# The stores of an FFT's first stage: one per pair of blocks in place of two

## The chip, the cores and the metric

The kernel runs on one core of a Trainium2 chip. The metric is the device time of one execution in microseconds (us), the median of several runs. The profile is that of one further execution.

The engines are TensorE (PE; its weight loads are PEld), VectorE (DVE), ScalarE (ACT), GpSimd (POOL) and SyncE (SP), which here only issues transfers. Each works through its own queue of instructions in order. ACT's queue holds arithmetic and the issues of transfers (DMAs) mixed.

## The reference

The input x has 2048 positions and 448 channels. It is normalised over the channels, and two branches of the result are added to it: a long convolution along the positions (an S4D state-space layer, whose kernel has 2048 taps per channel and comes from 256 modes), and a gated linear unit with 1792 hidden columns.

```python
x = A_u
xn = _layernorm(x, axis=-1)
# branch A: K from the modes, then a causal convolution by FFT of length 4096
P = jnp.exp((A * dt[:, None])[:, :, None] * pos[None, None, :])
K = 2.0 * jnp.einsum("dn,dnl->dl", C, P).real
Kf, Uf = jnp.fft.rfft(K, L2), jnp.fft.rfft(u_t, L2)
y = jnp.fft.irfft(Uf * Kf[None, :, :], L2)[:, :, :L]
# branch B
h = _sigmoid(xn @ w_gate) * (xn @ w_up)
return x + (y + xn * D_skip) + h @ w_down
```

## The kernel before, in words

**Two branches at once.** Two generators are advanced in turn: conv() (L1020) for branch A and glu() (L731) for branch B. They share all engines. The framework then orders the instructions of each engine with a scheduler that estimates how long each takes; tc.issue_after and high_priority (hp) bind a few of them. So an edit of one transfer can move instructions on every engine.

**Positions.** The 2048 positions are taken as 16 blocks of 128 rows. Normalised blocks are called xn (first 8) and xt (last 8).

**The first stage of x.** The 4096-point transform of x is done in two steps. In the first, x_first_stage (L277) multiplies one group g of 32 rows of a block by a table wx, which gives 64 spectral rows. It does so for a pair of blocks, b and b+1: block b into the upper 64 rows of a PSUM tile, block b+1 into the lower 64. ACT copies the tile to SBUF, and DMAs issued from ACT store it to x1_d in DRAM, laid out as (half of the channels, row(b, g), 64 spectral rows, 224 channels). row(b, g) (L274) is 32 * (b // 4 % 2) + 8 * g + 4 * (b // 8) + b % 4, so b and b+1 of a pair stand next to each other, and g and g+1 stand 8 apart.

- x_spec (L283) does this for the pairs of blocks 0 to 7, four calls. Two groups share a buffer (x1a, x1b, x1c in turn); the copies are L294 and L296, the stores L301.
- pair_first (L681) does it for the pairs of blocks 8 to 15, four calls, one group at a time; the copies are L689, the stores L691.

**The second step** reads x1_d much later, from 514 us on, in spectra() (loads at L875, issued from SP), and multiplies the spectra of x and K.

**K.** prep (L345) computes the modes' magnitudes and phases on ACT and DVE in 112-row tiles, at the same time as x_spec. kgen (L461) then takes the channels in 56 steps: a matmul makes phases (tr, L542), ACT turns them into sines and cosines in four instructions (S, L548 to L551), DVE multiplies by magnitudes me and mf (Et at L602 and L603, Ft at L604), TensorE contracts Ft with Et into ko (L616), and every fourth step a first stage of K's own transform follows (kp, kq, L566; stored by L574 from ACT).

**Branch B.** Weights are loaded from SP (wraw, L640 and L642; one buffer), cast on ACT to a rounded part wh (L760), and DVE takes the rest wl (L764), which also frees wraw for the next load. Rounded part and rest are multiplied apart. gate (L696) makes two PSUM banks (L710); ACT takes a tanh (th, L718), DVE forms hf (L721), ACT rounds it (hh, L726), DVE takes the rest (hl, L728). The down projection po (L823) follows, drained by DVE into acc (L828). All banks called gu and po are four buffers used in turn. While the last group of hidden columns of the first half is done, pair_norm, pair_turn (transposes L212, with copies xh and xr on ACT, L218, L221 and L224, and rests xl and xr on DVE, L219, L222 and L225) and pair_first are woven in for blocks 8 to 15.

**Transfers.** All DMAs issued from SP and ACT take eight completion semaphores in turn, in the order in which the scheduler puts them, and an issue waits until the DMA that had its semaphore before has landed.

Of the kernel before, what the change touches and what calls it, by code (L numbers as in the profile page):

```python
# [39 lines left out]
H = D // 2  # L40
# [90 lines left out]
def s4d_glu_kernel(ctx, tc, io):  # L131
    nc = tc.nc
# [9 lines left out]
    x1_d = dram.tile([2, NB, 64, H], F32, name="x1_d")  # L142
# [131 lines left out]
    def row(b, g):  # L274
        return 32 * (b // 4 % 2) + 8 * g + 4 * (b // 8) + b % 4

    def x_first_stage(to, xn, g):  # L277

        s = slice(32 * g, 32 * g + 32)
        for i in range(2):  # L280
            nc.tensor.matmul(to[64 * i : 64 * i + 64], wx[s], xn[i][s], start=True, stop=True)

    def x_spec(xn, b0):  # L283

        x1s_ = []
        for _ in range(2):
            x1s_.append(slots[("x1a", "x1b", "x1c")[x1s[0] % 3]])
            x1s[0] += 1
        ps = psc[-1].tile([128, 2, 512], F32, name="tr", bufs=1)
        kk = [psc[-1].tile([128, 512], F32, name=n, bufs=1) for n in ("ko", "kp")]  # L290
        with tc.issue_after(glu_mm[0].ins):
            for j in range(4):
                x_first_stage((ps[:, j] if j < 2 else kk[j - 2])[:, :D], xn, j)
        nc.scalar.copy(x1s_[0], ps[:, :, :D])  # L294
        for j in range(2):
            nc.scalar.copy(x1s_[1][:, j], kk[j][:, :D])  # L296
        for p in range(2):
            for i in range(2):
                r = row(b0 + i, 2 * p)
                for h in range(2):  # L300
                    nc.scalar.dma_start(  # L301
                        x1_d[h, r : r + 9 : 8].rearrange("r k d -> k r d"),
                        x1s_[p][64 * i : 64 * i + 64, :, H * h : H * h + H],
                    )
        yield 2 * WX

    def exp(ex, ki, fr, pl):
# [373 lines left out]
    def pair_first(b, xns):  # L681

        x1 = pg.tile([128, 2, D], F32, name="x1", tag="wraw", bufs=1)
        pss = [psg.tile([128, 512], F32, name="gu", bufs=4) for _ in range(4)]
        for g in range(4):
            x_first_stage(pss[g][:, :D], xns, g)
        for g in range(4):
            to = x1[:, g] if g < 2 else pg.tile([128, D], F32, name="x1", tag="rd", bufs=RB)
            nc.scalar.copy(to, pss[g][:, :D])  # L689
            for i in range(2):  # L690
                nc.scalar.dma_start(  # L691
                    x1_d[:, row(b + i, g)].rearrange("h k d -> k h d"),
                    to[64 * i : 64 * i + 64].rearrange("k (h d) -> k h d", h=2),
                )

    def gate(w, xs, to, between=None, behind=False):  # L696
        wh, wl = w
# [33 lines left out]
    def glu():  # L731
        for half in range(2):
# [4 lines left out]
            for fs_ in ORDER[half]:  # L737
# [8 lines left out]
                if cross:  # L746
                    xts = {b: pair_load(b) for b in range(8, 16, 2)}
                    step = lambda f_, b: f_(b, xts[b])
                    mid = [(pair_norm, 8), None, (pair_first, 8), (pair_first, 10)]
                    end = [(), ((pair_turn, 8), (pair_norm, 10)), ((pair_turn, 10), (pair_norm, 12)), ((pair_turn, 12), (pair_norm, 14))]  # L750
                    downs = {(0, 0): (pair_first, 12), (0, 1): (pair_turn, 14), (0, 3): (pair_first, 14)}
# [268 lines left out]
    def conv():  # L1020
        with tc.tile_pool(name="psk", bufs=1, space=PSUM) as ps_, tc.tile_pool(
# [9 lines left out]
            with tc.tile_pool(name="pst", bufs=1, side="right", reuse_waits="tile") as pst:  # L1031
# [54 lines left out]
                while preps:  # L1086
                    for p in list(preps):
                        try:
                            with tc.issue_after(hfs[max(0, len(hfs) - LAG)].ins):
                                next(p)  # L1090
                        except StopIteration:
                            preps.remove(p)
                    yield WP
                    n += 1
                    if n in (2, 3):
                        if n == 2:
                            slots["x1c"] = pst.tile([128, 2, D], F32, name="x1c", tag="raw1")
                        for b in range(0, 4, 2):
                            yield from x_spec([xns[n - 2][:, b + i] for i in range(2)], 4 * (n - 2) + b)
# [19 lines left out]
    while any(g is not None for g in gens):  # L1119
# [3 lines left out]
        i = min(live, key=lambda i: done[i] / total[i])  # L1123
# [33 lines left out]
```

## Time and profile before

| | us |
|---|---|
| median of 3 runs | 721.07 (721.0 to 723.01) |
| profiled execution | 721.87 |
| its span | 720.1 |
| TensorE, DVE, ACT, POOL busy | 670.9, 551.4, 428.0, 371.5 |
| mean granted TensorE clock | 0.984 |

The profile gives, for each instruction, its start from the beginning of the span, its length, its line in the kernel, and the tiles that it writes and reads (out<-in). Where an engine stood idle ahead of an instruction, the time and what ended it stand in brackets. "ACTq" and "SPq" rows are issues on an engine's queue, which are not counted as busy time of the engine. Names are cut at digits: x1_d is shown as x_d, x1 as x.

### The profile page before, as it was taken

What the parts mean: (1) busy time and instruction counts of PE and PEld (TensorE: products, weight loads), DVE (VectorE), ACT (ScalarE), POOL (GpSimd) and SP (SyncE); (2) the same over time, 40 slices, a digit from 0 to 9 for tenths busy, and PEclk for the clock granted to TensorE, in tenths of its full rate; (3) what the DMA queues carried; (4) which work ended last, traced back from release to release, by engine and by line L of the source; (5) the groups of instructions that cost most, each with busy time, mean ns of one, the idle gap of its engine ahead of it and who ended that gap; (6) DMA issues with size and microseconds to landing.
All of it is one profiled execution on the core that took longest, in us unless ns stands there. A gap on an engine that the chain in (4) does not pass through costs nothing.

```text
span 720.1 us, 19127 instructions
## 1 busy us (share of the span) xinstructions
PE 670.9 (93%) x7752; PEld 527.3 (73%) x7752; DVE 551.4 (77%) x766; ACT 428.0 (59%) x678; POOL 371.5 (52%) x431
## 2 busy tenths in 40 slices
PE   3898999999997997989999999999999999998995
PEld 2676888877876875656888788877877777776783
DVE  5899988699899889985879889987946555546543
ACT  3655975677787789965686877777542322313320
POOL 2100147766987988885676687577833002251001
PEclk9999999999999999999999999999999999999998
DMA  9947374554254453647933344141359988899645
GB/s 208 238 118 215 97 214 154 166 159 153 64 168 140 135 135 107 178 136 203 257 112 95 95 132 128 46 140 43 86 162 319 216 235 231 253 290 228 172 131 152
DMA packets 94503, 117.23 MB, mean 163 GB/s; under 512 B 12752, under 2 KB 78288, under 8 KB 94416
## 3 DMA queue, kind: packets, MB, share of 16 engines
q1 hardware_dynamic: 65904, 91.87, 45.3%
q10 hardware_dynamic: 25936, 18.24, 9.5%
q0 software_dynamic: 2576, 5.90, 3.1%
q8 instruction: 61, 1.00, 0.6%
q14 instruction: 26, 0.21, 0.1%
HBM read 72.13 MB, written 43.84 MB: 161 GB/s over the span
## 4 chain that ended last, share of the span: by engine, by line
PE 42%; DVE 6%; ACT 4%; DMA 3%; issue 2%; SPq 1%; POOL 0%; POOLq 0%; DVEq 0%; ACTq 0%
PE gu L710 16%; PE po L823 9%; PE sp L904 6%; PE pv L931 4%; PE ko L616 4%; PE tr L542 2%; DVE Ft L604 1%; DMA sx<-x_d 1%; DVE Et L602 1%; DMA out_dram<-ac 1%; DVE Et L603 1%; PE kp L566 1%; ACT S L551 1%; ACT S L548 1%; SPq L492 1%
## 5 line engine op out<-in xcount | busy, mean ns | idle before, releaser
L520 POOL TENSOR_TENSOR me<-me,pm 128x32 f32<-128x32 f32 (+1 forms) x168 | 142.4, 848 | 73.4 <-DVE Et L603 62.1
L520 POOL TENSOR_TENSOR mf<-mf,pm 128x64 f32<-128x64 f32 (+1 forms) x112 | 119.7, 1069 | 5.9
L710 PE MATMUL gu<-xh,wh 128*128 128x512 f32 x336 | 100.0, 406 | 0.7 <-ACT xh L221 0.7
L710 PE MATMUL gu<-xh,wl 128*128 128x512 f32 x336 | 97.0, 395 | 0.0
L710 PE MATMUL gu<-xl,wh 128*128 128x512 f32 x336 | 95.8, 391 | 0.0
L602 DVE TENSOR_TENSOR Et<-me,S 128x1024 f32<-128x1024 f32 x56 | 81.8, 1461 | 17.2 <-ACT S L551 16.1
L603 DVE TENSOR_TENSOR Et<-me,S 128x1024 f32<-128x1024 f32 x56 | 78.0, 1394 | 12.6 <-ACT me L533 10.5
L823 PE MATMUL po<-dh,hh 128*128 128x448 f32 x224 | 84.2, 376 | 2.6 <-DVE hf L721 2.2
L823 PE MATMUL po<-dl,hh 128*128 128x448 f32 x224 | 82.3, 367 | 0.0
L604 DVE TENSOR_TENSOR Ft<-mf,S 128x1024 f32<-128x1024 f32 x56 | 78.1, 1394 | 5.4 <-ACT S L551 2.7
L548 ACT ACTIVATE S<-tr 128x1024 f32<-128x1024 f32 x56 | 57.6, 1028 | 40.8 <-PE tr L542 40.4
L823 PE MATMUL po<-dh,hl 128*128 128x448 f32 x224 | 81.2, 367 | 0.0
L616 PEld LDWEIGHTS ko<-Et,Ft 128*32 128x32 f32 x3584 | 55.2, 112 | 31.4 <-DVE Ft L604 13.3
L710 PEld LDWEIGHTS gu<-xh,wh 128*128 128x128 f32 x336 | 61.8, 191 | 20.1 <-issue 5.1
L616 PE MATMUL ko<-Et,Ft 128*32 128x64 f32 x3584 | 65.6, 224 | 10.8 <-DVE Ft L604 9.9
L710 PEld LDWEIGHTS gu<-xh,wl 128*128 128x128 f32 x336 | 63.8, 190 | 14.5 <-DVE hf L721 0.7
L710 PEld LDWEIGHTS gu<-xl,wh 128*128 128x128 f32 x336 | 63.4, 189 | 13.5
L726 ACT CAST hh<-hf 128x512 fp32r<-128x512 f32 x56 | 34.9, 623 | 61.8 <-DVE hf L721 57.7
L721 DVE SCALAR_TENSOR_TENSOR hf<-th,gu 128x512 f32<-128x512 f32 x56 | 38.1, 680 | 39.5 <-PE gu L710 27.1
L551 ACT ACTIVATE S<-S,hpi 128x1024 f32<-128x1024 f32 x56 | 65.5, 1170 | 0.0
L787 POOL TENSOR_TENSOR dl<-rd,dh 128x448 fp32r<-128x448 f32 x14 | 24.8, 1769 | 78.1 <-ACT dh L786 67.6
L828 DVE SCALAR_TENSOR_TENSOR acc<-po,acc 128x448 f32<-128x448 f32 x80 | 48.1, 615 | 20.7 <-PE po L823 20.4
(208 smaller groups left out, 1299.7 us busy)
## 6 DMA issues: line engine op xcount, KB each, us to landing
sk_d<-sk ACTq DMA_DIRECT2D x14, 512.0 KB
sx<-x_d SPq DMA_DIRECT2D x32, 224.0 KB
skl<-sk_d SPq DMA_DIRECT2D x16, 448.0 KB
vp<-v_d SPq DMA_DIRECT2D x16, 448.0 KB
v_d<-vt SPq DMA_DIRECT2D x14, 448.0 KB
ph<-ph_d SPq DMA_DIRECT2D x224, 24.0 KB
wt_d<-wh SPq DMA_DIRECT2D x9, 512.0 KB
wt_d<-wl SPq DMA_DIRECT2D x9, 512.0 KB
```

What stands on the lines that cost most here:

```text
L520: ins = nc.gpsimd.tensor_tensor(m[:, :, w + a : 2 * w : n], m[:, :, a:w:n], par(base + i).unsqueeze(2).to_broadcast([128, 4 * DC, w // n]) ...
L548: nc.scalar.activation(rows(cs), pv, AF.Abs)
L551: sins[:] = [nc.scalar.activation(cs, cs, AF.Sin, scale=-TWO_PI, bias=hpi)]
L602: v.tensor_tensor(Et[:, :, :, 32:64], two(me[:, :, 32:64]), S[:, 1::-1], ALU.mult)
L603: v.tensor_tensor(Et[:, :, :, 0:32], two(me[:, :, 0:32]), S[:, 1:3, :, ::-1], ALU.mult)
L604: fts[:] = [v.tensor_tensor(Ft, two(mf), S[:, 3:5], ALU.mult)]
L616: mm = nc.tensor.matmul(ko[32 * j : 32 * j + 32, sl], Ft[:, cc, DC * h + 4 * q + j], Et[:, cc, DC * h + 4 * q + j], start=(k == 0), stop=( ...
L710: glu_mm[:] = [nc.tensor.matmul(ps, a_, b_, start=(n == 0), stop=(n == len(mm) - 1))]
L721: marks[1] = v.scalar_tensor_tensor(hf, th, 1.0, pgu[1], ALU.add, ALU.mult)
L823: glu_mm[:] = [nc.tensor.matmul(po, a_[:, bs], w_, start=(n == 0), stop=(n == 3 * fc - 1))]
L828: v.scalar_tensor_tensor(acc[:, b], po, 0.5, acc[:, b], ALU.mult, ALU.add)
L904: mm = nc.tensor.matmul(to, tb[:kk, t, 64 * c : 64 * c + 64], rhs, start=True, stop=True, skip_group_check=True,)
```

## The change

Each store takes both blocks of a pair, that is all 128 rows of the buffer, in place of 64. In x_spec a store still takes two groups and one half of the channels, in pair_first one group and both halves. There are 16 + 16 stores in place of 32 + 32, of 224 KB in place of 112 KB each. Layout of x1_d, loads and arithmetic are the same.

```diff
 # x_spec
         for p in range(2):
-            for i in range(2):
-                r = row(b0 + i, 2 * p)
-                for h in range(2):
-                    nc.scalar.dma_start(
-                        x1_d[h, r : r + 9 : 8].rearrange("r k d -> k r d"),
-                        x1s_[p][64 * i : 64 * i + 64, :, H * h : H * h + H],
-                    )
+            r = row(b0, 2 * p)
+            for h in range(2):
+                to = x1_d[h].rearrange("(g r) k d -> g r k d", r=8)[r // 8 : r // 8 + 2, r % 8 : r % 8 + 2]
+                nc.scalar.dma_start(to.rearrange("g i k d -> (i k) g d"), x1s_[p][:, :, H * h : H * h + H])
 # pair_first
             nc.scalar.copy(to, pss[g][:, :D])
-            for i in range(2):
-                nc.scalar.dma_start(
-                    x1_d[:, row(b + i, g)].rearrange("h k d -> k h d"),
-                    to[64 * i : 64 * i + 64].rearrange("k (h d) -> k h d", h=2),
-                )
+            r = row(b, g)
+            nc.scalar.dma_start(
+                x1_d[:, r : r + 2].rearrange("h i k d -> (i k) h d"), to.rearrange("p (h d) -> p h d", h=2)
+            )
```

The scheduler also orders other instructions anew. In the rows below, lines of the changed kernel behind x_spec are lower by 3, behind pair_first by 4.

ACT in the fourth call of x_spec (66 to 72 us of the profile), before: the copies, the stores and prep's hdt, fr and ki. The cast of the next weights (wh, L760) stands six rows further on.

```order
L294 COPY x1ab<-tr 128x896
L296 COPY x1ab<-ko 128x448
L296 COPY x1ab<-kp 128x448
L301 DMA x_d<-x1ab 64x2x224
L358 ACTIVATE hdt<-ex 112x2 x4
L301 DMA x_d<-x1ab 64x2x224
L364 ACTIVATE fr<-ex,hdt 112x256 x2
L364 ACTIVATE ki<-ex,hdt 112x256
L726 CAST hh<-hf 128x512
L364 ACTIVATE ki<-ex,hdt 112x256
L358 ACTIVATE hdt<-ex 112x2 x4
L301 DMA x_d<-x1ab 64x2x224
```

The same place on ACT in the changed kernel.

```order
L294 COPY x1ab<-tr 128x896
L296 COPY x1ab<-ko 128x448
L756 CAST wh<-wraw 128x1024
L301 DMA x_d<-x1ab 128x2x224
L296 COPY x1ab<-kp 128x448
L301 DMA x_d<-x1ab 128x2x224
L355 ACTIVATE hdt<-ex 112x2 x4
L301 DMA x_d<-x1ab 128x2x224
L361 ACTIVATE fr<-ex,hdt 112x256 x2
L361 ACTIVATE ki<-ex,hdt 112x256 x2
L355 ACTIVATE hdt<-ex 112x2 x4
L301 DMA x_d<-x1ab 128x2x224
```

The wh cast has moved up between the copies, and the four stores shown here are all there are.

DVE at the same time (53 to 64 us), before: prep's reciprocals of m and polynomial pl, the rest wl of the weights ahead of those above, and hf.

```order
L326 RECIPROCAL m_379<-m_379 112x128 x3
L728 TENSOR_TENSOR hl<-hf,hh 128x512
L326 RECIPROCAL m_379<-m_379 112x128
L326 RECIPROCAL m_391<-m_391 112x128 x4
L320 SCALAR_TENSOR_TENSOR pl<-pl,fr 112x514 x2
L260 SCALAR_TENSOR_TENSOR z<-z,ve 128x8
L764 TENSOR_TENSOR wl<-wraw,wh 128x1024
L721 SCALAR_TENSOR_TENSOR hf<-th,gu 128x512
```

The same place on DVE in the changed kernel.

```order
L323 RECIPROCAL m_379<-m_379 112x128 x2
L724 TENSOR_TENSOR hl<-hf,hh 128x512
L323 RECIPROCAL m_379<-m_379 112x128 x2
L323 RECIPROCAL m_391<-m_391 112x128
L760 TENSOR_TENSOR wl<-wraw,wh 128x1024
L323 RECIPROCAL m_391<-m_391 112x128 x3
L317 SCALAR_TENSOR_TENSOR pl<-pl,fr 112x514 x2
L260 SCALAR_TENSOR_TENSOR z<-z,ve 128x8
L717 SCALAR_TENSOR_TENSOR hf<-th,gu 128x512
```

wl has moved ahead of three reciprocals and pl; what stands ahead of hf is the same. Eight rows on, at the hf of 67.96 us, the next wl, too, comes to stand directly behind hf, ahead of the drains of po (acc).

ACT in the second call of pair_first and the pair_turn beside it (304 to 311 us), before: the copies of x1, those of the transposes (xh), the stores, and the S chain of a step of kgen.

```order
L689 COPY x_3811<-gu 128x448
L689 COPY x_3815<-gu 128x448
L218 CAST xh<-gu 128x2x256
L691 DMA x_d<-x_3811 64x2x224 x2
L221 CAST xh<-gu 128x256
L691 DMA x_d<-x_3815 64x2x224
L726 CAST hh<-hf 128x512
L691 DMA x_d<-x_3815 64x2x224
L548 ACTIVATE S_1123<-tr 128x2x2x256
L549 ACTIVATE S_1123<-tr 128x2x2x256
```

The same place on ACT in the changed kernel.

```order
L686 COPY x_3789<-gu 128x448
L686 COPY x_3792<-gu 128x448
L218 CAST xh<-gu 128x2x256
L688 DMA x_d<-x_3789 128x2x224
L688 DMA x_d<-x_3792 128x2x224
L545 ACTIVATE S_1107<-tr 128x2x2x256
L221 CAST xh<-gu 128x256
L546 ACTIVATE S_1107<-tr 128x2x2x256
L547 ACTIVATE S_1107<-tr 128x512
L548 ACTIVATE S_1107<-S_1107,hpi 128x2x512
L530 ACTIVATE me_1101<-me_1101 128x32x8
L722 CAST hh<-hf 128x512
```

The S chain has moved ahead of the second xh and of hh, which now comes last. On TensorE the phase matmul tr of the step after it moves up with it, ahead of a part of ko.

## The prediction

> **What bounds the kernel now.** I read the page first: the span, the busy line and the shares of the chain of waits.
>
> ```profile
> span 720.1 us, 19127 instructions
> PE 670.9 (93%) x7752; PEld 527.3 (73%) x7752; DVE 551.4 (77%) x766; ACT 428.0 (59%) x678; POOL 371.5 (52%) x431
> PE 42%; DVE 6%; ACT 4%; DMA 3%; issue 2%; SPq 1%; POOL 0%; POOLq 0%; DVEq 0%; ACTq 0%
> ```
>
> TensorE is busy for 670.9 of 720.1 us, so the time can fall only where TensorE stands still or runs at a lower clock, 49.2 us of idle in all. ACT, whose queue the change relieves, has 4% of the chain and its issuing (ACTq) none. So the question is how much of TensorE's idle time hangs on ACT's queue. The view of busy time by stretch shows it for the two places where the changed stores are issued: x_spec's lie in 42 to 78 us, pair_first's in 278 to 340 us.
>
> ```profile
> 42.00:78.00 36.00, 33.66 (x195) 24.90 (x194) 35.47 (x72) 23.22 (x47) 1.34 (x2) 1.00 0.64 174
> 78.00:110.00 32.00, 32.00 (x150) 26.46 (x149) 28.99 (x46) 25.48 (x53) 10.74 (x9) 1.00 0.57 174
> 278.00:312.00 34.00, 31.90 (x559) 19.93 (x559) 30.76 (x35) 30.98 (x52) 29.14 (x31) 0.95 0.55 159
> 312.00:340.00 28.00, 25.66 (x288) 18.01 (x285) 20.79 (x30) 17.62 (x30) 18.50 (x25) 0.94 0.55 153
> ```
>
> The columns are length, then busy time of PE, PEld, DVE, ACT and POOL, the granted clock and the DMA share. In the first place TensorE idles 2.34 us and DVE 0.53 us: DVE is full, ACT is not (23.22 of 36). Behind it, up to 110 us, TensorE idles 0.00. In the second place (62 us) it idles 2.10 + 2.34 = 4.44 us, and the clock is 0.95 and 0.94. What the change can win directly is therefore a few microseconds, under 1% of the span.
>
> **The issues themselves.** The view by line gives the cost of one issue on ACT's queue (minimum, median, maximum in ns).
>
> ```profile
> L301 ACTq DMA_DIRECT2D x_d<-x1ab x24: 582/614/1673, 44.3 to 73.7; - x24
> L301 ACTq DMA_DIRECT2D x_d<-x1c x8: 582/683/1182, 51.7 to 64.4; - x8
> L691 ACTq DMA_DIRECT2D x_d<-x x32: 582/600/2543, 281.6 to 334.6; - x32
> L574 ACTq DMA_DIRECT2D sk_d<-sk x14: 364/366/434, 178.1 to 533.1; - x14
> ```
>
> By the medians the 64 issues take 24 x 0.614 + 8 x 0.683 + 32 x 0.600 = 39.4 us of ACT's queue. A 128-row store with three dimensions isn't among them; the nearest row on the same queue is sk_d, 128 rows of 8 x 128 and 512 KB in 0.366 us. The other end is that an issue costs by the row: 2 x 0.600 = 1.2 us. sk_d has twice the rows of today's stores and 4.6 times their bytes and still costs less, so I take 0.366: 32 x 0.366 = 11.7 us. ACT's queue is rid of 27.7 us (at the other end of about 1). The bytes and the runs of 896 bytes stay as they are, so I put the movement of the data at no change. Most of the 27.7 us is worth nothing: an issue lies beside the arithmetic that ACT was given before it, and TensorE waits for little of it.
>
> **First place, 42 to 78 us.** ACT's longest stay in issuing, then the two instructions for which TensorE waits here, and their DVE neighbours; last the SP issues that load the next weights.
>
> ```profile
> 54.95 3.67 ACTq L301 DMA_DIRECT2D x_d<-x1ab  x4
> 66.47 0.54 ACT L296 COPY x1ab<-ko 128x448 f32<-128x448 f32 x1
> 73.40 1.04 ACT L760 CAST wh<-wraw 128x1024 fp32r<-128x1024 f32 x1
> ...
> 63.72 0.47 PE L823 MATMUL po<-dh,hh 128*128 128x448 f32 x1 [1.89 <-DVE hf L721]
> ...
> 56.52 4.19 DVE L326 RECIPROCAL m<-m 112x128 f32<-112x128 f32 x5
> 61.84 1.23 DVE L764 TENSOR_TENSOR wl<-wraw,wh 128x1024 fp32r<-128x1024 f32 x1
> 62.98 0.69 DVE L721 SCALAR_TENSOR_TENSOR hf<-th,gu 128x512 f32<-128x512 f32 x1
> 67.96 0.68 DVE L721 SCALAR_TENSOR_TENSOR hf<-th,gu 128x512 f32<-128x512 f32 x1
> 69.65 1.68 DVE L828 SCALAR_TENSOR_TENSOR acc<-po,acc 128x448 f32<-128x448 f32 x3
> 77.65 0.69 DVE L389 SCALAR_TENSOR_TENSOR w<-w,s 112x512 f32<-112x512 f32 x1 [0.29 <-ACT w L379]
> 80.48 0.69 DVE L389 SCALAR_TENSOR_TENSOR w<-w,s 112x512 f32<-112x512 f32 x1 [1.01 <-ACT junk L381]
> ...
> 63.53 0.39 SPq L640 DMA_DIRECT2D wraw<-in_B_w_gate_dram  x1
> 68.48 1.12 SPq L642 DMA_DIRECT2D wraw<-in_B_w_up_dram  x2
> ```
>
> The four issues from 54.95 hold ACT for 3.67 us, and yet TensorE's only long wait, 1.89 us, is for hf at 62.98. That hf stands in DVE's queue behind five reciprocals and wl, with no DVE idle before it. The new order puts wl ahead of the last three reciprocals but leaves the same instructions ahead of hf, so hf comes no earlier and the 1.89 us stay: gain 0. DVE's two waits for ACT (0.29 + 1.01 = 1.30 us) can go, but DVE has 32.00 - 28.99 = 3.01 us of slack in 78 to 110 us and TensorE waits for nothing there: 0 on the path, 1.30 at best.
>
> The order also adds something. wl of the next weights now stands directly behind the hf of 67.96, ahead of the first drain of po (L828), and its wh cast on ACT moves from 73.40 to just behind the copy of 66.47. wl takes 1.14 us from its start to the next one's (61.84 to 62.98) and puts the first L828 at 67.96 + 0.68 + 1.14 = 69.8 or a little later, where it was at 69.65. TensorE waited for no drain here, so this costs 0 to 0.3 us. But wh needs the weights. They can be loaded earlier, because the wl before it (61.84) now comes earlier by three of the five reciprocals, 3 x 0.84, and by the 1.13 us between their end and its start, 3.7 us in all: SP's loads move from 63.53 to about 59.8, their last issue ends at 65.9 in place of 69.60. Landing takes an unknown time beyond that; if it is 2 us, wh can start at 67.9 and end at 68.9, where DVE wants it at 67.96 + 0.68 = 68.6. That is 0.3 us more. I take 0.6 us as the cost of this place, 0 and 1.0 as its ends.
>
> **Second place, 278 to 340 us.** Here one issue does stop ACT, and the stop can be followed to TensorE.
>
> ```profile
> 304.51 0.43 SPq L775 DMA_DIRECT2D wl<-wt_d  x1
> ...
> 304.56 0.58 ACTq L691 DMA_DIRECT2D x_d<-x  x1
> 304.82 0.62 ACT L218 CAST xh<-gu 128x512 fp32r<-128x512 f32 x1
> 305.19 2.54 ACTq L691 DMA_DIRECT2D x_d<-x  x1
> 307.77 0.37 ACT L221 CAST xh<-gu 128x256 fp32r<-128x256 f32 x1 [2.33 <-PE po L823]
> 309.15 1.02 ACT L548 ACTIVATE S<-tr 128x1024 f32<-128x1024 f32 x1
> ...
> 312.00 1.05 ACT S L551
> ...
> 313.13 1.86 DVE L604 TENSOR_TENSOR Ft<-mf,S 128x1024 f32<-128x1024 f32 x1 [1.55 <-PE tr L542]
> ...
> 316.75 0.44 PE L212 MATMUL gu<-ident,xt 128*128 128x128 f32 x2 [0.94 <-DVE xr L225]
> 318.04 1.60 PE L616 MATMUL ko<-Et,Ft 128*32 128x64 f32 x50 [0.85 <-DVE Et L602]
> ...
> 318.00:320.00 2.00, 1.97 (x51) 1.79 (x52) 1.92 (x4) 1.49 (x3) 1.53 (x2) 0.55 0.43 99
> 320.00:322.00 2.00, 2.00 (x14) 1.49 (x16) 1.89 (x2) 0.00 (x0) 0.03 (x1) 0.60 0.39 88
> ```
>
> The store of 305.19 takes 2.54 us to issue, just after SP has put two weight loads on the DMA queues. The view blames po for ACT's 2.33 us of idling, but the interval is that of the issue. The S chain (L548 to L551) therefore starts only at 309.15, DVE's Ft waits 1.55 us (the chain of waits has S of L551, until 313.05, directly ahead of it), and TensorE waits 0.94 and 0.85 us for what DVE does behind that. After these two gaps the clock falls to 0.55 and 0.60: 1.97 x 0.45 + 2.00 x 0.40 = 1.69 us of TensorE's time.
>
> The new order has two issues behind L218 in place of four there, and the S chain directly behind them, ahead of xh (L221) and hh. If the long issue doesn't come back, S can start at 304.82 + 0.62 = 305.4, 3.7 us earlier. If it does in full, S starts at 307.7, still 1.4 us earlier. DVE's 1.55 us of waiting shrinks by 1.4 to all of it, and TensorE's 0.94 + 0.85 = 1.79 us by about as much: I take 1.5. What is late next is DVE itself, which is nearly full, so I book nothing beyond that. hh comes later by some 3 us; its first reader, po of the second half of the columns, stands many matmuls further on, so 0. With the two gaps down to 0.3 us the clock dip should go as well: 1.69. Together 3.2 us; 1.4 if the dip stays, 0 or a loss of the same size if the pieces of the new order meet other waits.
>
> The Trainium skill says of this dip, in "TensorE: Matmul & The Clock Gate", Part 1: The HAM clock gate, that the half clock comes after at least one idle window of about 3.4 us. By that rule gaps of 0.94 and 0.85 us cost no clock, and the sum would be 1.5 - 0.6 = 0.9 us of gain. The trace doesn't agree: the clock fell to 0.55 right behind them.
>
> **The sum.** -3.2 + 0.6 = -2.6 us. The profiled execution took 721.87 us (its span and 1.77 us around it), which becomes 719.3. It lies 0.80 us above the median of the three runs, 721.07, which becomes 718.5. A measurement of this kernel can tell about 0.3%, 2.2 us, from no change, so the forecast lies just outside.
>
> **The rivals.**
>
> *The issues were hidden anyway.* The long issue goes with SP's loads, not with the number of stores, so it returns and TensorE's gaps only move. For it: ACTq has 0% of the chain, and the 3.67 us at 54.95 cost TensorE nothing. Against it: S stands ahead of three casts now. Time: gain 0 to 0.6, about 720.8. A merged store that costs 1.2 us to issue, so that nothing is saved, comes out here too.
>
> *The dip has another cause.* The gap shrinks by 1.5 us but the clock still falls, as it would if the idle time before it counted: 721.07 - 1.5 + 0.6 = 720.2.
>
> *Slower: ACT stands at the wh cast.* If the weights of the first place are not there when ACT reaches the cast at 66.9, ACT waits in order, with the last copies of x_spec behind it, and DVE waits at wl with the drains of po behind it, while TensorE has four banks and then stops. If the loads stay where they are (last issue ends 69.60, 2 us to land), wh ends at 72.7 and wl starts 4.1 us late, in a stage where DVE idles 0.53 of 36 us. With a clock dip like the one above (1.69) it costs 5.8 us, and with the second place's 3.2 us gained the time is 721.07 + 5.8 - 3.2 = 723.7. It decides when SP issues the loads: at 63.5 it comes true, at 60 not.
>
> *A second gap closes.* TensorE waits 2.79 us for hf shortly before the second place, and the clock dips behind that too.
>
> ```profile
> 278.66 0.97 PE L281 MATMUL gu<-xt,wx 32*64 32x448 f32 x4 [2.79 <-DVE hf L721]
> 279.00:282.00 3.00, 3.00 (x58) 1.53 (x58) 3.00 (x5) 3.00 (x7) 2.11 (x3) 0.77 0.08 29
> 282.00:285.00 3.00, 2.31 (x38) 0.80 (x30) 3.00 (x4) 3.00 (x7) 1.53 (x2) 0.66 0.68 190
> ```
>
> That gap and dip are 2.79 + 3.00 x 0.23 + 2.31 x 0.34 = 4.3 us. If the earlier start of the preparation carries through to here, they go on top: 714.2. Against it: the order of TensorE, DVE and ACT from 130 to 275 us is the same in both programs, and DVE is full before that hf.
>
> **How the numbers follow.** Forecast 0.48 (its own range 716.6, with DVE's 1.30 us and the dearer place at no cost, to 720; three quarters of it are beyond 0.3%). Hidden anyway 0.20, dip stays 0.11, slower 0.15, second gap 0.06. Faster: 0.36 + 0.06 = 0.42. Same: 0.12 + 0.20 + 0.11 = 0.43. Slower: 0.15. The range goes from 714.0, which takes in the second gap, to 723.5, which leaves out the upper half of the slower rival.
>
> **What would show it.** Right: 32 stores at about 0.37 us each on ACTq; TensorE still waits 1.9 us for hf near 63 us; no wait of 0.9 us near 316 and 318 us and a clock of 1.00 there; 312 to 340 us shorter by about 3 us. Wrong: issues of 0.6 us or more; a wait of ACT's wh cast for wraw and TensorE idle near 70 us (slower rival); a new wait of TensorE for xr, Et or Ft between 300 and 340 us.

## The result, and the profile after

The changed kernel takes 717.93 us (median of 20 runs, 715.58 to 723.49); the kernel before, beside it, 723.12 us (20 runs, 718.24 to 728.20). The ratio is 0.9933, with a 95% interval of 0.9914 to 0.9951: faster by 4.8 us (3.5 to 6.2). The forecast was 2.6 us and 718.5 us; the 718.5 hung on a median of before from three runs, 721.07, which lies 2.05 us under that of the twenty. The profiled execution took 717.89 us.

The page of the profile after:

```profile
span 716.1 us, 19096 instructions
PE 671.3 (94%) x7752; PEld 528.2 (74%) x7752; DVE 550.8 (77%) x766; ACT 428.7 (60%) x678; POOL 378.8 (53%) x431
```

The issues of the merged stores, by line (minimum, median and maximum in ns):

```profile
L301 ACTq DMA_DIRECT2D x_d<-x1ab x12: 366/372/565, 44.5 to 68.4; - x12
L301 ACTq DMA_DIRECT2D x_d<-x1c x4: 366/430/512, 51.2 to 58.8; - x4
L688 ACTq DMA_DIRECT2D x_d<-x x16: 366/373/1846, 286.1 to 334.4; - x16
```

By the medians the 32 issues take 12 x 0.372 + 4 x 0.430 + 16 x 0.373 = 12.2 us where 11.7 were predicted. (Lines of the changed kernel: x_spec's store is L301, pair_first's L688.) A long issue, 1.85 us, is still among them, and it stands in the same call of pair_first as the one of 2.54 us before; S follows the start of xh by 2.20 us all the same:

```profile
308.35 0.66 ACT L218 CAST xh<-gu 128x512 fp32r<-128x512 f32 x1
308.60 1.85 ACTq L688 DMA_DIRECT2D x_d<-x  x1
310.55 1.03 ACT L545 ACTIVATE S<-tr 128x1024 f32<-128x1024 f32 x1 [1.53 <-DVE Et L600]
```

TensorE's waits that answer to those of the prediction, from the timeline:

```profile
63.81 0.74 PE L819 MATMUL po<-dh,hh 128*128 128x448 f32 x1 [2.91 <-DVE hf L717]
...
318.87 0.74 PE L539 MATMUL tr<-sel,ph 128*128 128x512 f32 x2 [0.39 <-ACT S L547]
320.37 0.64 PE L613 MATMUL ko<-Et,Ft 128*32 128x64 f32 x28 [0.76 <-DVE Et L599]
```

hf comes at the same time as before (63.08 against 62.98 us), but TensorE now reaches it earlier and waits 2.91 us in place of 1.89. Near 318 us the two waits of 0.94 and 0.85 us have become 0.39 and 0.76.

Two executions drift against each other, so the same microsecond is not the same work. As landmarks I take the casts of hh on ACT, 56 in each program and always in the same order, and cut the span at the starts of the 26th, 37th, 46th and 53rd. Busy time by these stretches, before and then after (length, PE, PEld, DVE, ACT, POOL, granted clock, DMA share):

```profile
0.00:279.18 279.18, 252.80 (x2573) 203.80 (x2573) 243.80 (x355) 195.85 (x314) 155.83 (x177) 0.99 0.56 156
279.18:425.25 146.07, 140.36 (x2092) 105.98 (x2089) 121.38 (x134) 112.10 (x173) 103.40 (x123) 0.98 0.52 150
425.25:529.23 103.98, 100.51 (x1617) 82.60 (x1615) 88.36 (x89) 72.08 (x103) 73.10 (x84) 0.98 0.34 99
529.23:649.26 120.03, 117.04 (x938) 88.49 (x926) 63.52 (x122) 32.83 (x62) 33.14 (x40) 1.00 0.90 245
```

```profile
0.00:282.02 282.02, 254.83 (x2571) 206.81 (x2573) 243.69 (x355) 196.53 (x313) 156.43 (x177) 0.97 0.54 155
282.02:426.43 144.41, 140.57 (x2093) 105.20 (x2090) 122.86 (x134) 112.20 (x173) 102.55 (x123) 0.98 0.51 152
426.43:528.01 101.58, 98.69 (x1615) 81.26 (x1614) 87.40 (x89) 72.00 (x103) 80.53 (x84) 1.00 0.34 101
528.01:645.60 117.59, 116.17 (x932) 88.25 (x923) 62.66 (x122) 32.85 (x62) 33.26 (x40) 1.00 0.91 249
```

The first stretch, with the first place in it, is 2.8 us longer; the second, with the second place, 1.7 us shorter; the third 2.4 and the fourth 2.4 us shorter, although no changed store is issued there. What of this belongs to the change, and what to the one execution, the experiments had to tell.

### The profile page after: what moved, and what is told of

It reads as the page before. It is cut to its first block, busy times and chain, and to the rows that moved or that the text cites. A ratio compares the mean times of both kernels' runs of the same rounds, so it can differ in the third digit from the quotient of the medians.

```text
span 716.1 us, 19096 instructions
## 1 busy us (share of the span) xinstructions
PE 671.3 (94%) x7752; PEld 528.2 (74%) x7752; DVE 550.8 (77%) x766; ACT 428.7 (60%) x678; POOL 378.8 (53%) x431
## 4 chain that ended last, share of the span: by engine, by line
PE 71%; DVE 13%; ACT 4%; issue 3%; SPq 3%; DMA 3%; POOL 1%; ACTq 0%; POOLq 0%; DVEq 0%
PE gu L706 29%; PE po L819 17%; PE sp L900 7%; PE ko L613 6%; PE pv L927 4%; PE tr L539 4%; SPq L489 2%; DVE Et L599 1%; PE gu L281 1%; DVE Ft L601 1%; DVE Et L600 1%; DMA acc<-in_A_u_dram 1%; DMA ph<-ph_d 1%; DVE pm L453 1%; DVE hl L724 1%
## 5 line engine op out<-in xcount | busy, mean ns | idle before, releaser
L517 POOL TENSOR_TENSOR me<-me,pm 128x32 f32<-128x32 f32 (+1 forms) x168 | 145.1, 864 | 67.6 <-DVE Et L600 56.8
L517 POOL TENSOR_TENSOR mf<-mf,pm 128x64 f32<-128x64 f32 (+1 forms) x112 | 121.3, 1083 | 6.1
L601 DVE TENSOR_TENSOR Ft<-mf,S 128x1024 f32<-128x1024 f32 x56 | 80.1, 1430 | 6.5 <-PE ko L613 4.0
```

What stands on the lines that cost most here:

```text
L517: ins = nc.gpsimd.tensor_tensor(m[:, :, w + a : 2 * w : n], m[:, :, a:w:n], par(base + i).unsqueeze(2).to_broadcast([128, 4 * DC, w // n]) ...
L601: fts[:] = [v.tensor_tensor(Ft, two(mf), S[:, 3:5], ALU.mult)]
```

## The experiments

All stretches together, one profile each (us):

| program | to 26th hh | 26th to 37th | 37th to 46th | 46th to 53rd |
|---|---|---|---|---|
| before | 279.2 | 146.1 | 104.0 | 120.0 |
| before, again | 280.2 | 149.1 | 103.0 | 118.4 |
| x_spec merged alone | 280.2 | 149.1 | 102.8 | 120.2 |
| before, S ahead of hh | 280.1 | 147.2 | 103.3 | 120.5 |
| before, with the late order | 280.5 | 145.2 | 100.9 | 117.4 |
| 64 stores of 128 rows | 281.9 | 146.5 | 103.9 | 117.9 |
| pair_first merged, hh ahead of S | 281.7 | 144.6 | 104.5 | 117.8 |
| pair_first merged, late order undone | 280.1 | 144.1 | 104.7 | 119.4 |
| pair_first merged alone | 279.2 | 144.0 | 101.4 | 118.5 |
| pair_first merged alone, again | 280.3 | 143.6 | 101.2 | 120.0 |
| after | 282.0 | 144.4 | 101.6 | 117.6 |
| after, again | 281.2 | 144.8 | 101.3 | 117.5 |
| pair_first merged, out off ACT | 283.4 | 145.9 | 101.1 | 116.3 |
| the same, again | 282.6 | 146.0 | 101.4 | 115.5 |

**One place at a time.** The first kernel keeps the hunk of x_spec alone, the second that of pair_first alone.

```diff
# against the changed kernel, x_spec merged alone:
-            nc.scalar.dma_start(x1_d[:, r : r + 2] ...)
+            for i in range(2):
+                nc.scalar.dma_start(x1_d[:, row(b + i, g)] ..., to[64 * i : 64 * i + 64] ...)
# pair_first merged alone:
-            for h in range(2):
-                nc.scalar.dma_start(..., x1s_[p][:, :, H * h : H * h + H])
+            for i in range(2):
+                for h in range(2):
+                    nc.scalar.dma_start(..., x1s_[p][64 * i : 64 * i + 64, :, H * h : H * h + H])
```

> x_spec's stores merged (16 of 128 rows), pair_first's 32 left as they were. Theory (the gain comes from the second place, 278 to 340 us, where ACT's long issue held the S chain; the first place gives nothing): no gain, 0 to +0.6 us against the kernel before (ratio 1.000 to 1.001), TensorE's wait for hf near 63 us 1.9 to 2.9 us, and the waits near 316 to 318 us still there. Rival (ACT's queue is worth something wherever it is relieved): about half of the measured 4.8 us, ratio 0.9967. Second rival (the merged stores of the first place lose time, through a clock dip behind the hf wait as in the changed kernel's profile): +2 to +3 us, ratio 1.003 to 1.004.

> pair_first's stores merged (16 of 128 rows), x_spec's 32 left as they were. Theory: the whole gain, -3.2 us (ratio 0.9956), and -5 to -6 us (0.992) if the loss that the changed kernel's profile shows at 63 to 70 us comes with the merged x_spec; TensorE's waits near 316 and 318 us below 0.5 us each and no clock dip there. Rival (relief counts by the number of stores): half, about -2.4 us, 0.9967. Second rival (a new order of the whole program, whatever it is, shifts the waits): anything between 0.990 and 1.005, with waits that differ far from the two places too.

x_spec alone: ratio 0.9993 (0.9968 to 1.0018). pair_first alone: 0.9933 (0.9907 to 0.9960), and in a second set of runs

> Only pair_first merged, once more, as the base of the two kernels beside it: 0.992 to 0.995 by its first runs (0.9933); 425 to 529 us in 101 to 102 us; no clock dip near 313 to 322 us. By the rival that its first runs were lucky: 0.996 or above.

0.9925 (0.9894 to 0.9956). So the gain is pair_first's, all of it within what can be measured; relieving ACT of 16 issues in the first place is worth nothing that these runs can tell (between -2.3 and +1.3 us), as predicted there. The wait for hf near 63 us is 2.90 us with x_spec merged alone and 1.95 with pair_first merged alone, so its length goes with x_spec, but its price is too small for the ratio to show.

**Fewer stores or more rows.** As many stores as before, but of 128 rows, each with half of the elements of a row.

```diff
# against the changed kernel
-                nc.scalar.dma_start(to.rearrange("g i k d -> (i k) g d"), x1s_[p][:, :, H * h : H * h + H])
+                for q in range(2):
+                    nc.scalar.dma_start(to[q].rearrange("i k d -> (i k) d"), x1s_[p][:, q, H * h : H * h + H])
...
-            nc.scalar.dma_start(x1_d[:, r : r + 2].rearrange("h i k d -> (i k) h d"), ...)
+            for h in range(2):
+                nc.scalar.dma_start(x1_d[h, r : r + 2].rearrange("i k d -> (i k) d"), to[:, H * h : H * h + H])
```

> Both places store 128 rows at a time, but each store takes only half of a row's 2 x 224 elements, so that there are 64 stores with the bytes and runs of before. Theory (an issue of 64 rows is dear by its shape, 0.6 us, and one of 128 rows takes 0.37 us whatever its bytes): 64 x 0.37 = 23.7 us of ACT's queue in place of 39.4, and most of the change's gain, ratio 0.993 to 0.997. Rival (the number of stores is what counts, 0.6 us each): 38 us of ACT's queue and a ratio of 1.000.

```profile
L690 ACTq DMA_DIRECT2D x_d<-x x32: 326/436/1717, 286.0 to 335.0; - x32
L302 ACTq DMA_DIRECT2D x_d<-x1ab x24: 326/408/737, 44.6 to 71.7; - x24
L302 ACTq DMA_DIRECT2D x_d<-x1c x8: 326/429/472, 51.5 to 60.7; - x8
```

By the medians this is 32 x 0.436 + 24 x 0.408 + 8 x 0.429 = 27.2 us of ACT's queue against 39.4 before: with two runs a row, a store of 64 rows was dearer to issue than one of 128. The ratio is 0.9982 (0.9956 to 1.0008), so anything from no gain to two thirds of the 4.8 us is possible; by its middle, a third of the issue time taken away brought about a quarter of the gain. This alone does not say that the time on ACT's queue is worth nothing, because the scheduler's order differs here from that of both kernels.

**Second profiles.** Both programs once more, to see which waits belong to the program.

> The changed kernel once more, for a second profile of the same program. If the program sets its waits: TensorE waits 2.9 us for hf near 63.8 us and 0.3 us for vt near 647 us again, each to 0.3 us, with a clock dip of 6 us behind the first. If they are an accident of the one execution: the wait near 647 us anywhere from 0.3 to 2.6 us, and dips of 3 or 6 us at other places, with 1 to 3 us more or less in the span.

> The kernel before once more, for a second profile. If the program sets its waits: 0.9 us for xr and 0.85 us for Et near 316 to 318 us again, 0.9 to 1.1 us for Ft near 466 us, 280 to 411 us taking 131 to 134 us. If they are an accident of the one execution: the long issue of 2.5 us near 305 us missing and S starting 2 to 3 us earlier behind xh, with the waits near 316 us below 0.5 us.

After, again: the wait for hf near 64 us is 4.49 us, and the wait for vt near 647 us (0.30 us in the first profile) is gone. Both scatter, and so does the fourth stretch: 117.4 to 120.5 us without regard to the stores. Before, again, at the second place on ACT:

```profile
306.38 0.62 ACT L218 CAST xh<-gu 128x512 fp32r<-128x512 f32 x1
306.75 0.62 ACTq L691 DMA_DIRECT2D x_d<-x  x1
...
309.16 0.62 ACT L726 CAST hh<-hf 128x512 fp32r<-128x512 f32 x1 [1.37 <-DVE hf L721]
309.16 0.58 ACTq L691 DMA_DIRECT2D x_d<-x  x1
309.79 1.02 ACT L548 ACTIVATE S<-tr 128x1024 f32<-128x1024 f32 x1
```

The issue that took 2.54 us takes 0.62 here, and S starts 3.41 us behind the start of xh, where it was 4.33. TensorE's waits near 316 and 318 us are gone too. Yet this stretch is 3.0 us longer. Busy time from 312 to 324 us, before again, and the same in the changed kernel:

```profile
312.00:324.00 12.00, 12.00 (x141) 7.28 (x132) 7.84 (x10) 8.41 (x15) 8.81 (x11) 0.57 0.33 78
```

```profile
312.00:324.00 12.00, 10.85 (x156) 6.30 (x156) 11.94 (x13) 12.00 (x21) 10.98 (x12) 1.00 0.45 151
```

TensorE doesn't wait at all in the first row, and loses 12.00 x 0.43 = 5.2 us to the clock; in the second it waits 1.15 us and loses none.

**Was it the order of S and hh?** The merged stores also brought S ahead of hh on ACT. Two kernels ask for this exchange by one edge each: pair_first merged with hh put back ahead of S, and the kernel before with S ahead of hh. (With the edge the scheduler moved other instructions of the second stretch too, on ACT and on DVE, so neither differs from its base in this pair alone.)

```diff
# pair_first merged, hh ahead of S: the 27th S is issued behind the 28th hh
+    tc.add_manual_dep(s_log[26].ins, h_log[27].ins.name, ...)
# before, S ahead of hh
+    tc.add_manual_dep(h_log[27].ins, s_log[26].ins.name, ...)
```

> The kernel of the run before with only pair_first merged, and one edge of issue order more: the S chain near 305 us (its Abs and what follows on ACT) is queued behind the cast of hh near 309 us, as it was in the kernel before. The 16 merged stores stay cheap. Theory now (the order of S and hh, which the fewer issues brought about, makes the gain): the gain goes, ratio 0.998 to 1.001, S starts 3 to 4.5 us behind the cast xh ahead of it, and TensorE waits 0.8 us or more near 316 to 320 us. Rival (the long issue of 2.54 us, which is gone with fewer stores, makes the gain): the gain stays, 0.992 to 0.995, since no issue of over 1 us stands ahead of S.

> The kernel before with its 64 stores of 64 rows, and one edge of issue order: the cast of hh near 308 us is queued behind the S chain near 309 us. Theory (order makes the gain): S starts 1 to 3.5 us behind xh, and the time falls by 1.5 to 4 us, ratio 0.9945 to 0.998, with no store changed. Rival (ACT's issue time makes the gain): ratio 0.999 to 1.001, since ACT still issues 64 stores and the long issue can stand there. A part beyond the place (the stretch from 412 to 494 us, 1.6 us shorter where pair_first is merged) stays as in the kernel before under either.

The first: 0.9979 (0.9952 to 1.0006), so most of the gain went, as the theory had it. The second: 0.9995 (0.9964 to 1.0026), no gain, as the rival had it. By the times alone one would say that both are needed. The stretches say something else:

```profile
281.70:426.34 144.64, 139.61 (x2092) 104.89 (x2093) 121.91 (x134) 112.65 (x174) 97.93 (x123) 0.98 0.51 152
426.34:530.85 104.51, 98.96 (x1616) 81.38 (x1615) 90.08 (x89) 71.86 (x103) 72.59 (x84) 1.00 0.33 98
```

With hh ahead of S the second stretch keeps its gain, 144.64 us. What is lost is in the third, 104.51 us, behind the last changed store: after the edge the scheduler had written the order of the kernel before for the rest of the program. So holding S back lost nothing where it should have, and S ahead of hh in the kernel before left that stretch at 147.2 us: the theory of S and hh does not hold. The long issue fell with the second profile of before, which is without it and yet longer there. These are one profile each; what all runs say follows below.

**The late order.** In the profile of before, DVE and TensorE near 461 us:

```profile
461.30 0.62 DVE L828 SCALAR_TENSOR_TENSOR acc<-po,acc 128x448 f32<-128x448 f32 x1 [0.92 <-PE po L823]
461.84 1.95 DVE L603 TENSOR_TENSOR Et<-me,S 128x1024 f32<-128x1024 f32 x1
463.71 1.33 DVE L602 TENSOR_TENSOR Et<-me,S 128x1024 f32<-128x1024 f32 x1
464.96 1.44 DVE L604 TENSOR_TENSOR Ft<-mf,S 128x1024 f32<-128x1024 f32 x1
...
466.45 1.04 PE L616 MATMUL ko<-Et,Ft 128*32 128x64 f32 x60 [0.94 <-DVE Ft L604]
```

A drain of po stands ahead of Et in DVE's queue and waits 0.92 us for TensorE; Et, Et and Ft stand behind it, and TensorE then waits 0.94 us for Ft. In the changed kernel and in pair_first merged alone, Et stands ahead of that drain; I call this the late order. Two kernels exchange the order of six pairs between 440 and 530 us, this one among them, and change no store: the kernel before with the late order, and pair_first merged with it undone (there the six edges give the order of the kernel before). The scheduler moved some neighbours of the six pairs along with them, on ACT and GpSimd too; outside this stretch DVE, ACT and GpSimd keep the order of the kernel that was edited.

```diff
# before, with the late order (et_a is L602, et_b L603, counted from 0)
+    for late, early in (
+        (et_b[44], acc_l[48]), (acc_l[54], et_b[46]), (hl_l[40], ft_l[48]),
+        (hfs[42], et_b[50]), (hl_l[42], et_a[50]), (acc_l[58], ft_l[52]),
+    ):
+        tc.add_manual_dep(late.ins, early.ins.name, ...)
```

> The kernel before, all 64 stores as they were, with six edges of issue order on DVE alone between about 440 and 530 us, taken from the order that the programs with merged pair_first stores have there. By the profiles so far the stretch between the casts of hh near 425 and near 529 us takes 102.7 to 104.6 us with the order of before and 101.0 to 101.6 with the other. Theory (that order alone is worth about 2.3 us, no store needs to change): the stretch takes 101 to 102 us, the wait of 0.9 us for Ft near 466 to 470 us goes, and the ratio is 0.995 to 0.998. Rival (the stretch is shorter only because of what the merged stores do before it): it stays at 103 to 104 us, ratio 0.999 to 1.001.

> Only pair_first merged, and in the same stretch six edges that put back the order of the kernel before. Theory: the stretch takes 103 to 104.5 us, 279 to 425 us stays at 144 to 146 us without a clock dip near 313 to 322 us, and the ratio is 0.995 to 0.998, 2 to 3 us above the program without the edges. Rival: stretch and ratio stay, 101 to 102 us and 0.992 to 0.995.

DVE in the kernel before with the late order:

```profile
460.44 0.61 DVE L831 SCALAR_TENSOR_TENSOR acc<-po,acc 128x448 f32<-128x448 f32 x1
460.98 1.21 DVE L605 TENSOR_TENSOR Et<-me,S 128x1024 f32<-128x1024 f32 x1
462.11 1.65 DVE L604 TENSOR_TENSOR Et<-me,S 128x1024 f32<-128x1024 f32 x1
463.68 0.61 DVE L831 SCALAR_TENSOR_TENSOR acc<-po,acc 128x448 f32<-128x448 f32 x1
464.26 1.51 DVE L606 TENSOR_TENSOR Ft<-mf,S 128x1024 f32<-128x1024 f32 x1
```

DVE waits no longer, nor does TensorE for that Ft. The second and third stretch of this kernel, then of pair_first merged with the late order undone:

```profile
280.53:425.76 145.23, 139.48 (x2092) 104.84 (x2089) 123.16 (x134) 112.49 (x173) 104.99 (x123) 0.99 0.52 151
425.76:526.64 100.88, 99.01 (x1617) 81.22 (x1615) 88.68 (x89) 71.83 (x103) 77.28 (x84) 1.00 0.34 100
```

```profile
280.05:424.12 144.07, 139.60 (x2093) 105.78 (x2090) 121.73 (x134) 112.38 (x173) 103.70 (x123) 0.98 0.50 152
424.12:528.80 104.68, 100.54 (x1615) 82.41 (x1614) 88.93 (x89) 71.78 (x103) 73.36 (x84) 0.98 0.33 98
```

The kernel before with the late order, no store changed: 0.9954 (0.9927 to 0.9981), 3.3 us. pair_first merged with it undone: 0.9957 (0.9934 to 0.9981), 3.1 us. Both together, beside them: 0.9925, 5.4 us. So the gain has two parts of about the same size, and only one of them needs the merged stores. In the table the third stretch takes 102.8 to 104.7 us in the seven profiles with the order of before (mean 103.7) and 100.9 to 101.6 in the seven with the late order (mean 101.2): 2.5 us, with no overlap. TensorE's idle time in it (length less PE) is 4.3 against 2.4 us on average. In the order of before TensorE waits for Ft twice there, 0.84 to 1.04 us and 1.59 to 1.96 us (near 466 and 494 us in the profile of before); in the late order the first wait is gone and the second is 0.50 to 1.18 us. Which of the six pairs does how much of this was not tried. The two kernels of 128 rows whose time hardly fell, 64 stores of 128 rows and hh ahead of S, both have the order of before here.

**Clock and the rest of the span, in all runs.** A profile is one execution, but the mean granted clock of every run is on record. Span x (1 - clock) is an estimate of what a run lost to the clock; the rest of the span is what is left. Means over the runs of each program (us; their standard errors are 0.3 to 1.2 for the loss and 0.2 to 0.6 for the rest):

| program | rows of pair_first's stores | order of the third stretch | runs | lost to the clock | rest of the span |
|---|---|---|---|---|---|
| before | 64 | before | 75 | 14.9 | 707.4 |
| x_spec merged alone | 64 | before | 12 | 15.0 | 706.8 |
| before, S ahead of hh | 64 | before | 12 | 15.6 | 706.1 |
| before, with the late order | 64 | late | 12 | 14.5 | 704.7 |
| 64 stores of 128 rows | 128 | before | 12 | 12.2 | 709.7 |
| pair_first merged, hh ahead of S | 128 | before | 12 | 12.1 | 708.7 |
| pair_first merged, late order undone | 128 | before | 12 | 11.8 | 707.4 |
| pair_first merged alone | 128 | late | 18 | 11.7 | 704.9 |
| after | 128 | late | 20 | 12.2 | 704.7 |
| pair_first merged, out off ACT | 128 | late | 13 | 11.3 | 703.5 |

The two parts of the gain stand apart here. Merging pair_first saves about 3 us of clock with either order of the third stretch (14.9 to 11.8 and 14.5 to 11.7), and the late order about 2.6 us of the rest with either form of the stores (707.4 to 704.7 and 707.4 to 704.9). The clock goes neither with S and hh (15.6 and 12.1) nor with the number of stores (12.2 with all 64). The rest is 1.3 and 2.3 us longer than before in the programs with hh ahead of S and with 64 stores of 128 rows, and that is why their times hardly fell; where these microseconds lie was not followed up.

**A version that may beat both.** ACT's th waits behind three stores of out near 640 us. In this kernel SP and GpSimd issue those first eight stores of out, and only pair_first is merged.

```diff
             eng = (nc.sync, nc.scalar, nc.gpsimd)[outs[0] % 3]
+            if outs[0] < 8:
+                eng = (nc.sync, nc.gpsimd)[outs[0] % 2]
```

> Only pair_first merged, and the eight stores of out near 640 us issued by SP and GpSimd alone, ACT's three taken away. If ACT's issuing there holds back th, hf and hh and with them TensorE: TensorE's wait for vt near 645 us (1.54 us in the profile without this edit, 0 to 2.6 us in the others) goes, another 1 to 2 us, ratio 0.990 to 0.992. Rival (th, hf and hh there are waited for only by DVE and the wait for vt comes from the v tables' DMA): no further gain, 0.993 to 0.994, and the wait stays or grows with GpSimd's four issues of 0.56 us behind its casts.

> Only pair_first merged, out's first eight stores issued by SP and GpSimd alone, once more, beside the program without that edit on the same chip. If ACT's issuing of out costs TensorE its wait for vt near 645 us: 1 to 2.5 us below it, ratio to before 0.989 to 0.992, and 529 to 649 us in 116 to 117 us. If the first 0.9909 was scatter: the same as the program beside it within 1 us.

0.9909 (0.9874 to 0.9944), and again 0.9895 (0.9858 to 0.9932). In the second set the median is 715.83 us, and 717.86 us for the same program without the edit beside it. The wait for vt, 1.83 us in that program's second profile, doesn't appear. Two microseconds is the point estimate; the intervals against before overlap, but the rest of the span, 703.5 against 704.9 us, points the same way. The fourth stretch, 116.3 and 115.5 us, is the shortest of all and says less than it seems to: the 53rd hh, its end, now comes earlier in TensorE's work (114.4 and 114.2 us busy in the stretch against 116.0 and more in all others). From the 46th hh to the end of the span the two profiles take 187.8 and 189.8 us, where the changed kernel takes about 188 in both of its own.

## Why the prediction was right or wrong, point by point

**The bound and the size.** TensorE is as busy after as before, and what was won is idle time and clock. The direction was right and the time, 717.93 us, near the forecast, but the sum is near for partly wrong reasons, and part of that is luck. The gain was 4.8 us and not 2.6; 718.5 came so close because the median that it was taken from was 2.05 us low. Nor was the prediction sure of the direction: it gave faster 0.42 and the same 0.43.

**The issues.** 0.37 us each was right. That most of the freed time is worth nothing held in the first place (x_spec merged alone).

**First place.** hf did come no earlier, the weights were loaded earlier (SP's first load at 59.98 us; 59.8 was predicted), and the cast of wh at 66.21 us waited for nothing: the slower rival didn't happen. What the prediction missed is that TensorE comes to the wait sooner and waits longer. A clock dip goes with it, 5.19 us busy at a clock of 0.50 in this execution:

```profile
63.00:69.00 6.00, 5.19 (x14) 4.64 (x15) 6.00 (x14) 5.07 (x13) 0.00 (x0) 0.50 0.64 188
```

The dip doesn't need the merged stores: before again has one of about 3.4 us there, with a wait of 1.92 us, and the program with hh ahead of S, whose x_spec is that of before, one of about 6.8 us. What the place costs on the median stays open between -2.3 and +1.3 us (x_spec alone); 0.6 was predicted. The first stretch scatters by 4.2 us among four profiles of programs that are the same up to its end (pair_first merged, with and without the edit on out: 279.2, 280.3, 283.4, 282.6), which is more than the place can cost.

**Second place.** The 3.2 us came out: the second stretch takes 147.4 us on average in the four profiles in which pair_first and its order are as before, and 144.7 in the seven with pair_first merged and its order, 2.7 us less; the run with the late order undone gives 3.1 us. The step that failed is the way there. Of the predicted 3.2 us, 1.5 were to be TensorE's two gaps, freed by S coming earlier when the 2.54 us issue goes. That issue was an accident of the one execution: before again is without it, and the profile after has one of 1.85 us in the same call. Moving S alone gained nothing, and holding S back lost nothing in that stretch. The gaps didn't go either: with pair_first merged alone TensorE still waits 1.43 us for Et near 317 us (1.15 us in two pieces in the profile after), and a new wait for Et was one of the prediction's own signs of being wrong.

```profile
316.64 0.64 PE L616 MATMUL ko<-Et,Ft 128*32 128x64 f32 x28 [1.43 <-DVE Et L602]
```

What went is the clock dip, which the prediction sized at 1.69 us from a profile in which it was short. By windows of 1 us the clock cost the second stretch 3.4, 7.9, 7.9 and 1.7 us in the four profiles with the order of before, and 1.7 to 3.6 in the seven: 5.2 against 2.7 on average, which is 2.5 of the 2.7 us. The difference lies behind 300 us: 1.7, 5.1, 5.1 and 0 us in the four, and 0 in each of the seven. Four profiles that differ so much would prove little, but all runs together say the same: with pair_first merged about 3 us less is lost to the clock.

Why the dip stays away is not settled, nor whether it is the stores themselves or the order of the second stretch that came with them. Before, TensorE has no gate or po matmul from 307.6 to 313.9 us, only tr, ko and those of L212 and L281; with pair_first merged alone the same gap is 308.6 to 313.3. But the profile of the kernel before with the late order has 6.3 us of it and no dip there, although this program loses nearly as much clock as before over its runs. An edit that moves only this was not tried.

**What was left out.** "I book nothing beyond that" was the other error: half of the gain is 90 us behind the last changed store. The prediction compared the two orders up to 275 us and at the two places, not behind them. There the drain ahead of Et could have been found in the profile of before (0.92 us of DVE's wait, 0.94 us of TensorE's), and the new order of the two would have shown that it goes.

**The rule that was weighed.** The Trainium skill, in "TensorE: Matmul & The Clock Gate", Part 1: The HAM clock gate, also says that the window of about 3.4 us runs freely, so that the moment of a transition varies. The runs agree: the same wait for hf near 280 us, 2.79 to 2.81 us long, comes with about 3.4 us at half clock in before and in pair_first merged alone, and with about 6.8 us in before again and after. By windows of 1 us the dips of before again begin at 63.8, 231.1, 278.9 and 313.0 us, and these lie 49, 14 and 10 lengths of 3.41 us apart. The condition weighed in the prediction, an idle window of that length, the runs don't show: before again fell to half clock at 313 us with no wait over 0.34 us in the 4 us ahead of it.

```profile
310.50 0.97 PE L281 MATMUL gu<-xt,wx 32*64 32x448 f32 x4 [0.24 <-DVE xl L219]
311.80 0.77 PE L616 MATMUL ko<-Et,Ft 128*32 128x64 f32 x40 [0.34 <-DVE Ft L604]
...
313.52 1.76 PE L281 MATMUL gu<-xt,wx 32*64 32x448 f32 x4
```

The last row takes 1.76 us for what took 0.97 three microseconds earlier.

## What to carry to other kernels

Where a scheduler writes the order, the edit is the whole new order: compare it to the end of the program, and look there for drains and loads that stand ahead of work which TensorE waits for. A long stop seen once in one profile is a candidate and no cause; take a second profile of the same program before building a sum on it, and use what is on record for every run (here the granted clock) to see whether it is there on average. And when an experiment's time agrees with the theory, see by landmarks where in the program the time went before believing it.

## What the runs showed that was not expected

- Issuing a store on ACT took longer for 64 rows of two runs (0.58 us at least) than for 128 rows of two (0.366) or of one (0.326).
- The clock fell to half in pieces of about 3.4 us (12.00 x 0.43 / 0.5 = 10.3 us, three of them, in the row of before again above). Dips of one, two and three such lengths came at the same place of the program, the wait near 280 us, in different executions. Each piece costs 1.6 to 1.7 us, a third of what the merged pair_first gains in all.
- Dips came with waits under 0.35 us ahead of them, and waits of 1.43 us came without a dip.
